# A fused attention and two feed-forward layers: P5 after P7 in FFN 1's slots, v loaded half a block earlier, one block's cosine taken unreduced, bounds in borrowed PSUM tiles, GpSimd passes cut in two

## The chip, the cores and the metric

The kernel runs on one NeuronCore of a Trainium2 chip. The metric is the device time of one execution in microseconds (us). The engines are TensorE (PE, with its weight loads shown as PEld), VectorE (DVE), ScalarE (ACT), GpSimd (POOL) and SyncE (SP), which here only issues DMAs. Each engine works through its own list of instructions in order; semaphores make an instruction wait for others. Matmuls write to PSUM, the accumulator memory; GpSimd works on SBUF only.

## The reference

Everything is float32, with N = 6016 tokens and C = 256 channels:

```python
qn = q / (norm(q, axis=1) + 1e-6);  kn = k / (norm(k, axis=1) + 1e-6)
a = softmax(kn.T @ qn / tau)          # 256 x 256: attention over channels
x = v @ a                             # 6016 x 256
h = x @ w_in1;  x = (h * cos(h)) @ w_out1        # FFN 1, d_ff = 2048
h = x @ w_in2;  out = (h * sigmoid(h)) @ w_out2  # FFN 2, d_ff = 2048
```

The weights come in as 64-bit words (seen as int64) that the kernel decodes to float32 itself.

## The kernel before, in words

**Precision.** A float32 number is split into a high part hi (fp32r, made by ScalarE's Copy) and a low part lo = x - hi (VectorE or GpSimd). A product is three passes, hi*hi, lo*hi and hi*lo (`PASSES`).

**Stages.** (1) Scores and softmax; the attention matrix is folded into `w_in1`, so that FFN 1 reads v directly. (2) FFN 1 of blocks 0 to 2, 24 units of 256 hidden columns: the 16 units of blocks 0 and 1 in turns (`TURNS`), then the 8 of block 2 (`FIRST`). A unit is 12 matmuls of 512 columns for h (`emit_h`, L727), a cosine, a split into hi and lo, and 12 matmuls into the output accumulator (`emit_o1`, L759), two units later. (3) FFN 1 of blocks 3 to 10, 8 slots each, in a Strassen-like form: seven products P1 to P7 of 128x256 per slot in place of eight (`first_layer`, L962), three passes each. Block 11 (`PLAIN`, 384 tokens) follows without that form. (4) FFN 2 of all blocks, seven products for both layers. Blocks are 512 tokens.

**The cosine.** Blocks 0 to 2 reduce the argument first: ScalarE writes k = round(h / 2 pi + 0.25) as an integer (L734), VectorE h - 2 pi k (L735), ScalarE the sine (L742), VectorE the product with h (L743). From block 3 on `cosine_in` takes the sine of h itself (L1221) times `small[b]`, which is 1 where a bound on |h| is below 1.5 and 0 otherwise, and VectorE multiplies (L1222). The bound is a small matmul (L426) of `most` (per channel, the largest |v| of a block; `span_of`, L399) and `widest` (the largest |w| of each row; L408, L417), reduced by VectorE (L430, L431). `every` gathers whether all bounds held (L432); it decides at the end whether a general version is run.

**A slot of FFN 1** (slot j; u is the pair whose products begin, p the one of slot j-1). In PSUM each pair has `ys` (y in half 1, the first sum in half 0) and `xz` (z in half 0, x in half 1). TensorE's order: P4 and P5 of p; P1 and P7 of u; the 12 output matmuls of the pair three slots back; P3 of p; P2 and P6 of u. ScalarE's: the split hi of slot j-2's pair (L1228), y <- x (L1276), p7 <- z (L1277), sine of xz (L1221), the slot's share of other work, sine of ys (L1221), u2 <- y (L1310). VectorE's: z += u2 and ys0 = y + p7 (L1012), the split lo (L1230), the product with xz (L1222), other work, the product with ys (L1222). P5 adds to y, and so waits until L1310 has copied y into u2:

```python
product(z, "P4", w, x, start=False)
product(y, "P5", w, x, start=False)   # waits for u2 <- y, the last work of ScalarE's slot
add(z, z, u2)
add(ys[k][:, 0], y, p7)
```

`p7` and `u2` are single tiles (`seeds`), used again in every slot.

**The other work** of a block's 8 slots is dealt out by `misc(b, m)`: at m = 0 and 4 a piece of `w_in2` or `w_out2` begins to be decoded (ACT L310, POOL L287), at 1 and 5 VectorE clamps it (L293, L294), at 2 and 6 VectorE and GpSimd finish it (L300, L303, L351), GpSimd splits it (L357, L358) and SP stores it (L1057). At m = 0 the v of the next block is loaded (`load_v`, L393, one buffer); at 1 to 3 it is formed and split for the seven products (POOL L906, ACT L913, L917); at m = 3 the span of v is taken, and FFN 1's finished block is copied (L825 to L827), formed (L848 to L852), split (L839, L843) and stored (L845) at m = 3 to 7. At m = 7 the next block's bound is computed into `xz`. While block 2 runs, GpSimd also forms and splits `w_in1` (A and B in `FORMING`, L929 to L944) and the v of block 3.

The order of each engine's list is the order of the code: nothing is scheduled afterwards. What a buffer's earlier reader or writer holds back waits by semaphore.

Of the kernel before, what the change touches and what calls it, by code (L numbers as in the profile page):

```python
# [217 lines left out]
def direct(ctx, tc, qk, vT, tau, w_in1, w_out1, w_in2, w_out2, outT, dp, kept, within):  # L218
# [1258 lines left out]
```

## Time and profile before

| | |
|---|---|
| median of 3 runs | 1082.03 us (1078.99 to 1083.86) |
| the profiled execution | 1083.9 us, of which 1082.1 us are the span from the first to the last instruction |
| mean granted TensorE clock | 0.980 |
| TensorE / VectorE / ScalarE / GpSimd busy | 94% / 82% / 72% / 38% of the span |

The busy shares are means over stages with different limits, so the stages have to be read one by one. TensorE's share counts matmuls at their modelled ends, and a matmul at a lower clock counts as longer.

### The profile page before, as it was taken

How to read it: one execution, taken by the hardware profiler on the slowest of the kernel's cores; microseconds unless marked ns; L12 is line 12 of the kernel's file. 1: busy time of each engine (PE TensorE's matmuls, PEld its weight loads, DVE VectorE, ACT ScalarE, POOL GpSimd, SP SyncE). 2: the span in 40 equal slices, each digit the busy share in tenths (PEclk: the TensorE clock that was granted, in tenths of full speed). 3: DMA queues.
4: the chain of work that ended last, by engine and by line, in shares of the span. 5: the costliest groups of instructions: out<-in, count | busy, mean ns of one | idle time of the engine just before them, and what ended most of it. 6: DMA issues, size and time to landing. Idle time of an engine off the chain costs nothing.

```text
span 1082.1 us, 18543 instructions
## 1 busy us (share of the span) xinstructions
PE 1015.9 (94%) x7060; PEld 945.6 (87%) x7060; DVE 891.4 (82%) x1241; ACT 783.5 (72%) x1381; POOL 413.5 (38%) x378
## 2 busy tenths in 40 slices
PE   9999998798989898898889999999999999999998
PEld 8778887687878787787878999999999999999998
DVE  6799889786878787787978568999999999999972
ACT  6886767575667666676756678888888888888863
POOL 4343358566666656566645201111111111111110
PEclk9999999898989998999999999999999999999999
DMA  9930035323233332323234985022202201220101
GB/s 350 350 125 1 1 151 229 146 88 117 89 120 124 131 142 76 140 88 117 89 112 163 364 344 185 11 79 89 87 12 79 89 27 70 81 89 12 54 22 37
DMA packets 35011, 126.58 MB, mean 117 GB/s; under 512 B 3170, under 2 KB 4450, under 8 KB 30178
## 3 DMA queue, kind: packets, MB, share of 16 engines
q1 hardware_dynamic: 34770, 125.12, 31.5%
q8 instruction: 57, 0.93, 0.4%
q14 instruction: 40, 0.33, 0.1%
q10 hardware_dynamic: 144, 0.20, 0.1%
HBM read 73.01 MB, written 52.30 MB: 116 GB/s over the span
## 4 chain that ended last, share of the span: by engine, by line
PE 63%; DVE 10%; POOL 9%; ACT 7%; DMA 6%; issue 4%; SPq 0%; POOLq 0%; ACTq 0%; DVEq 0%
PE o L962 19%; PE xz L962 12%; PE o L759 11%; PE ys L962 10%; DMA vraw<-vT_dram 5%; PE h L727 4%; DVE t L1222 2%; ACT hi L1228 2%; DVE lo L1230 2%; ACT t L1221 2%; POOL stage L358 2%; POOL t L843 2%; DMA qk<-qk_dram 1%; PE o L1002 1%; PE S L537 1%
## 5 line engine op out<-in xcount | busy, mean ns | idle before, releaser
L789 DVE TENSOR_TENSOR lo<-t,hi 128x768 fp32r<-128x768 f32 (+1 forms) x176 | 194.6, 1115 | 29.2 <-ACT hi L781 29.1
L759 PE MATMUL o<-hi,wo 128*128 128x512 f32 (+1 forms) x768 | 203.2, 389 | 0.3 <-ACT hi L748 0.3
L776 POOL TENSOR_TENSOR t<-t 128x256 f32<-128x256 f32 x88 | 64.4, 732 | 361.6 <-DVE t L773 317.7
L781 ACT ACTIVATE hi<-t 128x768 fp32r<-128x768 f32 (+1 forms) x176 | 168.9, 960 | 27.1 <-PE o L962 26.3
L759 PEld LDWEIGHTS o<-hi,wo 128*128 128x128 f32 x768 | 145.0, 198 | 18.2 <-ACT hi L748 0.9
L1230 DVE TENSOR_TENSOR lo<-t,hi 128x1024 fp32r<-128x1024 f32 (+1 forms) x72 | 113.3, 1573 | 44.1 <-ACT hi L1228 43.9
L962 PE MATMUL o<-hi,wo 128*128 128x256 f32 x770 | 134.7, 275 | 0.0
L1228 ACT ACTIVATE hi<-t 128x1024 fp32r<-128x1024 f32 (+1 forms) x72 | 74.6, 1037 | 72.7 <-DVE t L1222 64.4
L962 PE MATMUL ys<-xhi,wf 128*128 128x256 f32 x384 | 81.9, 296 | 45.9 <-ACT u L1310 45.4
L759 PE MATMUL o<-lo,wo 128*128 128x512 f32 (+1 forms) x384 | 116.1, 385 | 3.0 <-DVE lo L749 3.0
L962 PEld LDWEIGHTS ys<-xhi,wf 128*128 128x128 f32 x384 | 63.4, 192 | 61.8 <-ACT u L1310 58.1
L962 PEld LDWEIGHTS o<-hi,wo 128*128 128x128 f32 x770 | 117.0, 192 | 0.0
L962 PE MATMUL o<-lo,wo 128*128 128x256 f32 x385 | 105.9, 275 | 0.0
L759 PEld LDWEIGHTS o<-lo,wo 128*128 128x128 f32 x384 | 74.3, 195 | 14.5 <-DVE lo L749 4.0
L1222 DVE TENSOR_TENSOR t<-ys,t 128x512 f32<-128x512 f32 x64 | 43.8, 684 | 41.5 <-ACT t L1221 41.5
L1221 ACT ACTIVATE t<-ys,half_pi,small 128x512 f32<-128x512 f32 x64 | 49.7, 777 | 38.4 <-PE ys L962 38.2
L962 PE MATMUL xz<-xhi,wa 128*128 128x256 f32 x384 | 76.2, 281 | 0.4 <-ACT p L1277 0.4
L962 PEld LDWEIGHTS o<-lo,wo 128*128 128x128 f32 x385 | 73.9, 192 | 0.0
L1373 ACT ACTIVATE ys<-xz 128x256 f32<-128x256 f32 x88 | 32.4, 368 | 46.4 <-PE xz L962 45.5
L962 PE MATMUL xz<-x2hi,wf 128*128 128x256 f32 x352 | 65.8, 275 | 0.0
L962 PE MATMUL xz<-x2hi,wa 128*128 128x256 f32 x352 | 65.8, 275 | 0.0
L768 DVE TENSOR_TENSOR t<-t 128x512 f32<-128x512 f32 x88 | 60.2, 684 | 0.2 <-ACT t L1416 0.2
(250 smaller groups left out, 2987.0 us busy)
## 6 DMA issues: line engine op xcount, KB each, us to landing
qk<-qk_dram SPq DMA_DIRECT2D x22, 512.0 KB, 7.6
x2hi<-xshi SPq DMA_DIRECT2D x11, 896.0 KB, 5.1
x2lo<-xslo SPq DMA_DIRECT2D x11, 896.0 KB, 7.1
wi_dram<-stage SPq DMA_DIRECT2D x8, 1024.0 KB, 4.9
wo_dram<-stage SPq DMA_DIRECT2D x8, 1024.0 KB, 4.8
vraw<-vT_dram SPq DMA_DIRECT2D x11, 512.0 KB, 7.2
outT_dram<-q SPq DMA_DIRECT2D x22, 256.0 KB, 2.0
xshi<-t SPq DMA_DIRECT2D x10, 512.0 KB, 6.7
```

Of the source, the lines that this page charges most:

```text
L727: nc.tensor.matmul(hp[:, s, :n], lhsT, rhs, start=(i == 0), stop=(i == len(todo) - 1))
L759: nc.tensor.matmul(o[:, e, :n], wo1_at(i, f)[:, e * P : (e + 1) * P], columns(parts[k][:, s, :n]), start=(f == 0 and (i, k) == PASSES[0]), ...
L768: eng.tensor_tensor(out=t[:, 4:6, :c], in0=t[:, 0:1, :c].to_broadcast([P, 2, c]), in1=t[:, 1:3, :c], op=ALU.subtract)
L776: eng.tensor_tensor(out=t[:, 7, :c], in0=t[:, 3, :c], in1=t[:, 6, :c], op=ALU.subtract)
L781: nc.scalar.activation(hi[:, sl, :c], t[:, 1:][:, sl, :c], AF.Copy)
L789: nc.vector.tensor_tensor(out=lo[:, sl, :c], in0=t[:, 1:][:, sl, :c], in1=hi[:, sl, :c].bitcast(F32), op=ALU.subtract)
L962: nc.tensor.matmul(out, w(p, ka), columns(x[r][:, kb - 1]), start=(start and i == 0), stop=(stop and i == 2), skip_group_check=True,)
L1221: nc.scalar.activation(out, h, AF.Sin, bias=half_pi, scale=small[b])
L1222: nc.vector.tensor_tensor(out=out, in0=h, in1=out, op=ALU.mult)
L1228: nc.scalar.activation(hf, tf, AF.Copy)
L1230: nc.vector.tensor_tensor(out=lf, in0=tf, in1=hf.bitcast(F32), op=ALU.subtract)
L1373: nc.scalar.activation(y2, x2, AF.Copy)
```

## The change: what it does

- In FFN 1's slots of the seven-product form, P5 of the pair before, and the addition that reads it, come after P1 and P7 of the new pair.
- v of block b+2 is loaded at m = 4 of block b (before: of b+1 at m = 0); v of block 4 is loaded ahead of the first slot.
- Block 2's units take the sine of h itself (`cosine_in`). For that its bound is computed in unit 15: the span of v in unit 13, `widest` at the end of unit 14, the spans of the weights two units earlier (`SPANS` 6).
- The bounds of blocks 2 and 3 use the PSUM tile of the unit to come (`ready`), between the two halves of the output matmuls of units 15 and 22. Block 3's bound stood ahead of the first slot of stage 3 before.
- `small` is one tile with a column for each block; `every` is one minimum at the end in place of a product after each bound. The maximum of a bound stays in PSUM.
- GpSimd's larger subtractions and one addition are cut into two instructions: the split of decoded weights (896 columns into 512 and 384), of formed v (1024 into 2 x 512), of FFN 1's formed output from block 2 on, and of the forms of `w_in1`. The raw parts of 768 columns are left as they were.

```diff
-SPANS = 8
+SPANS = 6
...
-            nc.gpsimd.tensor_tensor(out=lo, in0=src, in1=hi.bitcast(F32), op=ALU.subtract)
+            for sl in (slice(0, 4), slice(4, NU)) if len(src.shape) == 3 else (slice(0, P),):
+                nc.gpsimd.tensor_tensor(out=lo[:, sl], in0=src[:, sl], in1=hi[:, sl].bitcast(F32), op=ALU.subtract)
...
-        s = small[b] = wp.tile([P, 1], F32, tag="small", name=f"small{b}", bufs=2)
-        nc.vector.tensor_reduce(out=s, in_=to, axis=AX.X, op=ALU.max)
-        nc.vector.tensor_scalar(out=s, in0=s, scalar1=LIMIT, scalar2=1.0, op0=ALU.is_le, op1=ALU.mult)
-        nc.vector.tensor_tensor(out=every, in0=every, in1=s, op=ALU.mult)
+        most_of_all = room[:, NS : NS + 1]
+        nc.vector.tensor_reduce(out=most_of_all, in_=to, axis=AX.X, op=ALU.max)
+        nc.vector.tensor_scalar(
+            out=small[b], in0=most_of_all, scalar1=LIMIT, scalar2=1.0, op0=ALU.is_le, op1=ALU.mult
+        )
...
-        hp = next_room().tile([P, 2, TB], F32, tag="h", name=f"h{b}_{m}")
+        hp = ready.pop() if ready else h_tile(f"h{b}_{m}")
...
         def low(kind, sl):
             hi, lo = places[kind]
-            eng.tensor_tensor(out=lo, in0=t[:, sl], in1=hi.bitcast(F32), op=ALU.subtract)
+            for k in (slice(0, 2), slice(2, 4)) if kind == "formed" and b >= 2 else (slice(None),):
+                eng.tensor_tensor(out=lo[:, k], in0=t[:, sl][:, k], in1=hi[:, k].bitcast(F32), op=ALU.subtract)
...
         hp = emit_h(u)
-        t = emit_first(i, u, hp)
+        bounded = {TURNS - 1: FIRST, TURNS + 6: FIRST + 1}.get(i)
+        if bounded is not None:
+            emit_o1(units[i - LAG], parts[i - LAG], (0,))
+            ready.append(h_tile(f"bound{bounded}"))
+            bound(bounded, ready[0][:, 0])
+        if i < TURNS:
+            t = emit_first(i, u, hp)
...
-        emit_cos(u, hp, t)
+        if i < TURNS:
+            emit_cos(u, hp, t)
+        else:
+            cosine_in(b, hp, flat(T[i % 2]))
...
+        if i == TURNS - 3:
+            span_of(FIRST, vraw)
         if i == TURNS - 2:
             split_v(FIRST, vraw)()
+            spread_weights()
...
-    raws = {}
+    raws = {FIRST + 2: load_v(FIRST + 2)}
...
     def misc(b, m):
-        if b < NB and m == 0:
-            raws[b + 1] = load_v(b + 1)
+        if m == 4 and b + 2 < NB:
+            raws[b + 2] = load_v(b + 2)
...
             product(z, "P4", w, x, start=False)
-            product(y, "P5", w, x, start=False)
             add(z, z, u2)
-            add(ys[k][:, 0], y, p7)
...
             product(x2, "P1", w_, x_, start=True)
             product(z2, "P7", w_, x_, start=False)
+        if p is not None and not pp_:
+            product(y, "P5", w, x, start=False)
+            add(ys[k][:, 0], y, p7)
...
-        if j == 0:
-            bound(FIRST + 1, next_room().tile([P, 2, TB], F32, tag="h", name="bound")[:, 0])
```

What this moves on the engines. TensorE, from P6 of one slot to the output matmuls of the next (block 5, slots 1 and 2), before; `xz1`, `ys1` are the older pair's tiles, `xz0`, `ys0` the newer one's:

```order
L962 MATMUL ys1_1473<-xhi5_1904,wf0_1026 128x256 x2
L962 MATMUL ys1_1473<-xlo5_1905,wf0_1026 128x256
L962 MATMUL xz1_1474<-xhi5_1904,wa0_89 128x256 x2
L962 MATMUL xz1_1474<-xlo5_1905,wa0_89 128x256
L962 MATMUL ys1_1473<-xhi5_1904,wf0_1026 128x256 x2
L962 MATMUL ys1_1473<-xlo5_1905,wf0_1026 128x256
L962 MATMUL xz0_1425<-xhi5_1904,wa1_90 128x256 x2
L962 MATMUL xz0_1425<-xlo5_1905,wa1_90 128x256
L962 MATMUL xz0_1425<-xhi5_1904,wf1_1027 128x256 x2
```

The pairs of rows are P6, P4, P5, P1 and the start of P7. The same place on TensorE in the changed kernel:

```order
L976 MATMUL ys1_1465<-xhi5_1902,wf0_1031 128x256 x2
L976 MATMUL ys1_1465<-xlo5_1903,wf0_1031 128x256
L976 MATMUL xz1_1466<-xhi5_1902,wa0_89 128x256 x2
L976 MATMUL xz1_1466<-xlo5_1903,wa0_89 128x256
L976 MATMUL xz0_1423<-xhi5_1902,wa1_90 128x256 x2
L976 MATMUL xz0_1423<-xlo5_1903,wa1_90 128x256
L976 MATMUL xz0_1423<-xhi5_1902,wf1_1032 128x256 x2
L976 MATMUL xz0_1423<-xlo5_1903,wf1_1032 128x256
L976 MATMUL ys1_1465<-xhi5_1902,wf0_1031 128x256 x2
L976 MATMUL ys1_1465<-xlo5_1903,wf0_1031 128x256
```

P5 (the last two rows) now stands behind P1 and P7. SP's list over block 3, before (`vraw5` is block 5's v, asked for when block 4 begins, behind the stores of block 2's output):

```order
L393 DMA vraw4_1437<-vT_dram 128x2x512
L1057 DMA wi2_dram0_1546<-stage_1031 128x2048
L267 DMA raw_wi22_1548<-w_in2_dram 128x2x256
L845 DMA xshi2_1594<-hi0_501 128x768
L845 DMA xslo2_1595<-lo0_503 128x768
L1057 DMA wi2_dram1_1751<-stage_1031 128x2048
L267 DMA raw_wi23_1753<-w_in2_dram 128x2x256
L845 DMA xshi2_1594<-t0_499 128x1024
L845 DMA xslo2_1595<-t1_500 128x1024
L393 DMA vraw5_1853<-vT_dram 128x2x512
```

And SP's list there in the changed kernel:

```order
L395 DMA vraw4_1416<-vT_dram 128x2x512
L1071 DMA wi2_dram0_1543<-stage_1036 128x2048
L268 DMA raw_wi22_1545<-w_in2_dram 128x2x256
L395 DMA vraw5_1639<-vT_dram 128x2x512
L853 DMA xshi2_1592<-hi0_502 128x768
L853 DMA xslo2_1593<-lo0_504 128x768
L1071 DMA wi2_dram1_1752<-stage_1036 128x2048
```

The load has moved past four stores, one store of decoded weights and one load. VectorE in block 2's units 16 and 17, before (`h2_0` is block 2's first h):

```order
L735 SCALAR_TENSOR_TENSOR t0_499<-t0_499,h2_0_1076 128x1024
L749 TENSOR_TENSOR lo1_504<-t1_500,hi1_502 128x1024
L743 TENSOR_TENSOR t0_499<-h2_0_1076,t0_499 128x1024
L417 TENSOR_REDUCE widest_100<-largest_99 128x2
L420 MEMSET every_101 128x1
L735 SCALAR_TENSOR_TENSOR t1_500<-t1_500,h2_1_1117 128x1024
L749 TENSOR_TENSOR lo0_503<-t0_499,hi0_501 128x1024
L743 TENSOR_TENSOR t1_500<-h2_1_1117,t1_500 128x1024
```

And VectorE from the end of unit 14 to unit 16 in the changed kernel, where h of block 2's first unit stands in `bound2`:

```order
L419 TENSOR_REDUCE widest_100<-largest_99 128x2
L431 TENSOR_REDUCE bound2_1059<-bound2_1059 128x1
L432 TENSOR_SCALAR smalls_102<-bound2_1059 128x1
L742 SCALAR_TENSOR_TENSOR t1_501<-t1_501,h1_7_1040 128x1024
L756 TENSOR_TENSOR lo0_504<-t0_500,hi0_502 128x1024
L750 TENSOR_TENSOR t1_501<-h1_7_1040,t1_501 128x1024
L756 TENSOR_TENSOR lo1_505<-t1_501,hi1_503 128x1024
L1085 TENSOR_TENSOR t0_500<-bound2_1059,t0_500 128x1024
```

The reducing pass (L735) is gone from block 2's units, and the bound's two small instructions stand one unit ahead of them.

## Rows read from the trace of the kernel before

**Rows 1.** Busy time by stretch: bounds, length, PE, PEld, DVE, ACT, POOL, PEclk, DMA

```profile
144.78:198.42 53.64, 45.31 (x200) 38.01 (x198) 49.73 (x44) 37.39 (x41) 39.55 (x25) 0.95 0.59 229
198.42:245.17 46.75, 41.84 (x253) 36.91 (x253) 35.23 (x47) 30.23 (x54) 27.82 (x27) 0.95 0.25 91
245.17:543.80 298.63, 261.97 (x1598) 235.10 (x1597) 233.31 (x313) 196.51 (x342) 187.18 (x175) 0.95 0.32 112
543.80:586.54 42.74, 38.09 (x233) 34.01 (x232) 33.64 (x49) 28.97 (x51) 17.92 (x19) 0.96 0.46 164
586.54:626.20 39.66, 38.87 (x231) 37.07 (x230) 23.22 (x34) 22.35 (x35) 16.25 (x14) 1.00 0.80 302
626.20:1082.10 455.90, 450.77 (x3927) 450.02 (x3925) 394.55 (x629) 362.31 (x748) 64.42 (x88) 1.00 0.21 77
```

**Rows 2.** Waits over the span: total us, times, longest

```profile
PEld ys L962 <- ACT u L1310: 58.1, 64, 4.4
```

**Rows 3.** Timeline of TensorE, one slot (block 8): start, length, engine, line

```profile
471.69 0.49 PE L962 MATMUL ys<-xhi,wf 128*128 128x256 f32 x2 [0.20 <-ACT u L1310]
...
472.12 0.39 PE L962 MATMUL xz<-xhi,wa 128*128 128x256 f32 x2
...
472.80 1.03 PE L759 MATMUL o<-hi,wo 128*128 128x512 f32 x4
...
475.39 0.38 PE L962 MATMUL ys<-xhi,wf 128*128 128x256 f32 x2
...
476.39 0.39 PE L962 MATMUL xz<-xhi,wa 128*128 128x256 f32 x2
...
477.09 0.49 PE L962 MATMUL ys<-xhi,wf 128*128 128x256 f32 x2 [0.20 <-ACT u L1310]
```

**Rows 4.** Timeline of ScalarE, the end of the same slot

```profile
475.92 0.78 ACT L1221 ACTIVATE t<-ys,half_pi,small 128x512 f32<-128x512 f32 x1 [0.84 <-PE ys L962]
476.65 0.38 ACT L1310 ACTIVATE u<-ys 128x256 f32<-128x256 f32 x1
```

**Rows 5.** Timeline of VectorE, the same slot

```profile
471.33 0.69 DVE L1222 TENSOR_TENSOR t<-ys,t 128x512 f32<-128x512 f32 x1 [0.53 <-ACT t L1221]
...
473.15 1.23 DVE L1230 TENSOR_TENSOR lo<-t,hi 128x1024 fp32r<-128x1024 f32 x1 [0.40 <-ACT hi L1228]
474.38 0.69 DVE L1222 TENSOR_TENSOR t<-xz,t 128x512 f32<-128x512 f32 x1
```

**Rows 6.** Timeline of SP, ScalarE and TensorE, first slots of block 8

```profile
449.43 1.88 SPq L393 DMA_DIRECT2D vraw<-vT_dram  x1
...
457.35 0.90 ACT L913 ACTIVATE xhi<-vraw 128x768 fp32r<-128x768 f32 x1 [3.91 <-DMA vraw<-vT_dram]
...
459.24 0.79 PE L962 MATMUL ys<-xhi,wf 128*128 128x256 f32 x2 [3.71 <-ACT u L1310]
```

**Rows 7.** Timeline of GpSimd and VectorE; VectorE's groups from 245.17 to 543.80

```profile
496.53 2.38 POOL L843 TENSOR_TENSOR t<-y,t 128x1024 fp32r<-128x1024 f32 x1
...
497.50 2.48 DVE L1230 TENSOR_TENSOR lo<-t,hi 128x1024 fp32r<-128x1024 f32 x1 [0.46 <-ACT hi L1228]
...
L1230 DVE TENSOR_TENSOR lo<-t,hi 128x1024 fp32r<-128x1024 f32 x48 | 81.7, 1701 | 19.4 <-ACT hi L1228 19.2
...
L432 DVE TENSOR_TENSOR every<-every,small 128x1 f32<-128x1 f32 x7 | 11.2, 1598 | 0.2
```

**Rows 8.** Block 2: timeline of TensorE; VectorE's group from 144.78 to 198.42

```profile
178.25 0.70 PE L759 MATMUL o<-lo,wo 128*128 128x512 f32 x2 [2.12 <-DVE lo L749]
...
186.95 1.03 PE L727 MATMUL h<-xhi,wa 128*128 128x512 f32 x4
...
192.13 0.20 PE L426 MATMUL bound<-most,widest 128*128 128x4 bf16 x2
197.40 0.58 PE L1147 MATMUL ys<-wo 128*128 128x256 f32 x1 [5.06 <-DVE small L430]
...
L735 DVE SCALAR_TENSOR_TENSOR t<-t,h 128x1024 f32<-128x1024 int32 x9 | 10.9, 1215 | 3.4 <-ACT t L734 3.4
```

More of the change, by code (lines that the diff above doesn't have):

```diff
@@ L249, in direct @@
     every = wp.tile([P, 1], F32, name="every")
-    small = {}
+    smalls = wp.tile([P, NB], F32, name="smalls")
+    small = {b: smalls[:, b : b + 1] for b in range(NB)}
     class Weights:
@@ L419, in spread_weights @@
         )
-        nc.vector.memset(every, 1.0)
     def bound(b, room):
@@ L717, in quadrant, with h_tile @@
         return first[name, m][:, i] if (name, m) in first else w[:, i, NU]
+    ready = []
+    def h_tile(name):
+        return next_room().tile([P, 2, TB], F32, tag="h", name=name)
     def emit_h(u):
@@ L917, in raw_low, with formed_low @@
             nc.scalar.activation(hi[:, FORMED], formed, AF.Copy)
-        return [form, raw_low, lambda: sub(lo[:, FORMED], formed, hi[:, FORMED].bitcast(F32))]
+        def formed_low():
+            for k in (slice(0, 2), slice(2, 4)):
+                sub(lo[:, FORMED][:, k], formed[:, k], hi[:, FORMED][:, k].bitcast(F32))
+        return [form, raw_low, formed_low]
     formed_w1 = {}
@@ L928, in form_w1 @@
         hi, lo = [wa[k][:, i].bitcast(F32) for i in range(2)]
-        nc.gpsimd.tensor_tensor(out=base, in0=hi, in1=lo, op=ALU.add)
+        for m in range(2):
+            nc.gpsimd.tensor_tensor(out=base[:, m], in0=hi[:, m], in1=lo[:, m], op=ALU.add)
         q = base.rearrange("p m (s b) -> p m s b", b=P)
@@ L943, in split_w1 @@
         nc.scalar.activation(hi, t, AF.Copy)
-        nc.gpsimd.tensor_tensor(out=lo, in0=t, in1=hi.bitcast(F32), op=ALU.subtract)
+        for m in range(2):
+            nc.gpsimd.tensor_tensor(out=lo[:, m], in0=t[:, m], in1=hi[:, m].bitcast(F32), op=ALU.subtract)
     def w1_slot(m):
@@ L1067, in fetch, with cosine_in @@
         nc.sync.dma_start(out=to.bitcast(F32), in_=src[:, :, : to.shape[2]])
+    def cosine_in(b, h, out):
+        nc.scalar.activation(out, h, AF.Sin, bias=half_pi, scale=small[b])
+        nc.vector.tensor_tensor(out=out, in0=h, in1=out, op=ALU.mult)
     FIRST = 2
@@ L1101, in direct @@
             vraw = load_v(FIRST)
+        if i == TURNS - 3:
+            span_of(FIRST, vraw)
         if i == TURNS - 2:
             split_v(FIRST, vraw)()
+            spread_weights()
         if i == TURNS - 1:
             vraw = load_v(FIRST + 1)
-        if i == TURNS:
-            spread_weights()
         if SPANS <= i < SPANS + 8:
@@ L1116, in direct @@
                 {"A": form_w1, "B": split_w1}[what[0]](int(what[1]))
-        if i == TURNS + 5:
+        if i == TURNS + 4:
             span_of(FIRST + 1, vraw)
@@ L1122, in direct @@
             v = units[i - LAG]
-            emit_o1(v, parts.pop(i - LAG))
+            emit_o1(v, parts.pop(i - LAG), (0, 1) if bounded is None else (1,))
             if v[1] == NPAIR - 1:
@@ L1178, in seven @@
         return t.rearrange("p s c -> p (s c)").rearrange("p (i s e) -> p i s e", i=2, s=NU)
-    raws = {}
+    raws = {FIRST + 2: load_v(FIRST + 2)}
+    del vraw
     def misc(b, m):
-        if b < NB and m == 0:
-            raws[b + 1] = load_v(b + 1)
+        if m == 4 and b + 2 < NB:
+            raws[b + 2] = load_v(b + 2)
         if m in (0, 4):
@@ L1218, in bank @@
         return t.rearrange("p j c -> p (j c)")[:, :n]
-    def cosine_in(k, b, h, out):
-        nc.scalar.activation(out, h, AF.Sin, bias=half_pi, scale=small[b])
-        nc.vector.tensor_tensor(out=out, in0=h, in1=out, op=ALU.mult)
     def high_and_low(j, q, what):
@@ L1282, in first_layer @@
         elif p is not None:
-            cosine_in(k, p[1], xz[k], tq[:, 1])
+            cosine_in(p[1], xz[k], tq[:, 1])
         if j == 0:
@@ L1307, in first_layer @@
         if p is not None and not pp_:
-            cosine_in(k, p[1], ys[k], tq[:, 0])
+            cosine_in(p[1], ys[k], tq[:, 0])
         if not up:
@@ L1321, in tail_of_first @@
             late = [sp.tile([P, NU, HB], F32R, name=f"late{k}") for k in range(2)]
+            nc.vector.tensor_reduce(out=every, in_=smalls[:, FIRST:], axis=AX.X, op=ALU.min)
             nc.vector.tensor_copy(within, every[0:1])
```

## The prediction

> **What bounds the kernel now.** I read the busy times by stretch first, then the list of waits, then the timeline of one slot on three engines. The stretches [rows 1] divide the span. The last, FFN 2, is 455.90 us with TensorE busy for 450.77 at a granted clock of 1.00; no instruction of it is changed, so it stays. The change works between 144.78 (block 2's first unit) and 626.20 (FFN 2's first product). There TensorE has gaps, and the list of waits gives their owner: its weight loads wait 58.1 us, 64 times, for L1310, the copy u2 <- y [rows 2], once for each of the 64 slots of the seven-product form.
>
> An ordinary slot shows why [rows 3]. P5 starts at 471.69 and the next P5 at 477.09: a period of 5.40. The matmuls alone are shorter. P1 starts at 472.12 and P4 at 476.39, 4.27 later without a gap; P1 and P7 take 0.68 together (472.12 to 472.80), so a product takes 0.34, and with P4 and P5 a slot is 4.27 + 0.67 = 4.94. The other 0.46 is a loop: P5, P1, P7, the 12 output matmuls to 475.39, P3, then ScalarE's sine of ys at 475.92 and u2 at 476.65 [rows 4], then the next P5. Eight floors of 4.94 are 39.5 a block. Blocks 4 to 9 take 298.63 us [rows 1], 49.8 each. Of the 10.3 above the floor, eight loops are 3.7, and the first slots of a block give 3.7 more: v is asked for at 449.43, ScalarE waits 3.91 us for it at 457.35, and P5, which needs ScalarE's u2, has waited 3.71 at 459.24 [rows 6]. The remaining 2.9 is what follows the gap (the granted clock is 0.95 over these blocks and 1.00 in FFN 2, and the first two matmuls behind it take 0.79 against 0.49 in rows 3), and late VectorE work.
>
> VectorE is late where GpSimd is in its way. A lo takes 1.23 us alone [rows 5]; at 497.50 it takes 2.48, having met a GpSimd subtraction of 2.38 that began at 496.53 [rows 7]. Over 48 lo the mean is 1701 ns [rows 7], so the excess is 0.47 x 8 = 3.8 us a block. In the first stretch, block 2's, an undisturbed unit is 192.13 - 186.95 = 5.18 [rows 8], eight are 41.4; the stretch is 53.64 long.
>
> **The change part by part.**
>
> *P5 behind P7.* The loop loses P1 and P7: 5.40 - 0.68 = 4.72, under the floor of 4.94, so TensorE is what is late next and an ordinary slot gains 0.46. The price could be on the other side of P5: the addition that reads p7 now follows P7, and ScalarE may not write the next p7 before it. P5 would start 1.0 us after P4, and its three matmuls (0.34) and an addition shorter than the 0.69 of the 512-column product [rows 5] end by about 2.1. ScalarE's hi ends at about the same time (473.15, when lo begins [rows 5], is 2.1 after that slot's P4, which stands one period before 476.39 [rows 3]), and the copy of y stands between hi and p7: a margin of some tenths. I take nothing for it, with 0.3 a slot as the upper end.
>
> *v half a block earlier.* The one buffer is free by then, its last reader being VectorE's span at m = 3. In SP's list the load stands behind the m = 2 store of weights and ahead of the stores of FFN 1's output. v took 457.35 - 449.43 = 7.9 us to be usable [rows 6], and now has more than four slots (over 19 us). So the 3.7 us goes whole, and the low clock with it. For block 4's v, asked for just before the first slot, SP first has the stores of block 1's output; I leave 1 us of wait in block 3.
>
> *GpSimd's passes in two, and no product into `every`.* L432 goes, 11.2 us in the six blocks or 1.9 each [rows 7]. A lo that meets a pass waits for half as long at most, but there are more passes to meet. Bounds: nothing to 1.9 (half of 3.8) a block; I take 1. The additional passes cost GpSimd perhaps 0.1 us each; it is busy for 187.18 of 298.63 us, so that is hidden.
>
> Here a rule speaks against the change. The row at 497.50 shows that the lo ended 1.07 us after GpSimd's pass (499.98 against 498.91), as if it had begun then [rows 7]. The Trainium skill, "SBUF — State Buffer", section "Who interferes with whom", says that a VectorE instruction with two SBUF inputs and a GpSimd instruction that reads SBUF exclude each other for the whole instruction; the trace agrees, as the numbers before this sentence show. By that rule cutting a pass in two leaves the time for which the pair is taken as it was; that is the first rival.
>
> *Sum for a block.* TensorE's floor is 39.5. VectorE is busy for 233.31 / 6 = 38.9; less 1.9 for L432 and 1 for shorter meetings 36.0, and it idles 0.40 a slot for hi [rows 5], 3.2 in eight: 39.2. Both chains are so near each other that uneven slots (the forms of x2 and the clamp fall into m = 4 and 5, one after another) will show; I add 2.5 to the floor: 42.0 a block. Blocks 4 to 9: 6 x 7.8 = 46.6 saved. Block 10's first seven slots [rows 1]: 42.74 - 7 x 5.25 = 6.0. The stretch behind has one such wait and a few: 0.8. Block 3 (46.75) has three short slots, since its output matmuls are block 2's last two units: 4.38 + 3.64 + 3.64 + 5 x 4.94 = 36.4 as a floor (a product 0.335, 12 output matmuls 2.59 from rows 3); the VectorE chain makes the short ones about 1 us longer each, and with 1.1 for uneven slots and 1 for v it is 40.5: 6.2 saved.
>
> *Block 2.* Each of eight units loses one ScalarE and one VectorE pass (L735, 1215 ns [rows 8]); VectorE is busy for 49.73 of this stretch's 53.64 us [rows 1], and TensorE's waits there are for its lo (2.12 at 178.25 [rows 8]). With 9.7 us less it is no longer the bound. Block 3's bound stood between block 2 and block 3: TensorE did it at 192.13 and waited 5.06 us for VectorE's answer behind other work, up to 197.40 [rows 8]. Now it stands a unit earlier, between two halves of output matmuls, with the answer needed 1.3 us later. Block 2's own bound comes in unit 15, behind the span and the spread, which VectorE does in units that now have two more reductions; for a late answer there I allow from nothing to 1 us. Floor 41.4 + 0.44 (clear, P1) = 41.9; with 1.6 for the two bounds and the meetings with GpSimd, which is busy for 39.55 of the 53.64 us, 43.5: 10.1 saved. What GpSimd has left over (the last `w_in1` forms) is needed only by slot 6.
>
> *Total.* 10.1 + 6.2 + 46.6 + 6.0 + 0.8 = 69.7. The span would be 1012.4, the execution (1.8 us around the span) 1014.2. The profiled execution lies 1.9 above the median, so the forecast is 1012.3, say 1013.
>
> **The rivals.**
>
> *The pair of GpSimd and VectorE becomes the bound.* GpSimd's 31.2 us a block (187.18 / 6, some of it waiting) and VectorE's eight lo at 1.23 add to 41.0 without VectorE's decoding and forms. If these exclude each other wholly and instructions wait for each other besides, a block is 46: 22.6 saved in blocks 4 to 9, 3 in block 10, 3 in block 3, 7 in block 2; 1083.9 - 35.6 - 1.9 = 1046. For it: 41.0 is above 39.5. Against: GpSimd has 18.6 us a block in which it is not busy, and its results are needed a slot or more later. 0.12.
>
> *The wait moves to ScalarE.* p7 is one tile: L1277 now waits for the addition behind P5, the sines come late and with them u2. At 0.3 a slot, and a little for v's return, a block is 44.5: 6 x 5.3 + 4 + 4 + 10 = 50 saved, 1032. For it: the margin worked out above is a few tenths, and any late P5 uses it up. Against: ScalarE still has 0.84 of idle before the sine of ys [rows 4]. 0.15.
>
> *TensorE nearly at its floor.* Blocks of 40.3, block 3 at 38, block 2 at 42.5: 57 + 8.7 + 11.1 + 7.5 + 1 = 85 saved, 997. For it: the loop of 4.72 has slack in every slot, which can take up one late slot. Against: the two chains of 39.5 and 39.2. 0.15.
>
> *Slower.* GpSimd's chain falls behind the block. Its place is ScalarE's L310 at m = 0 and 4, which needs a buffer that GpSimd must first have emptied (two buffers for decoding and for formed v), and stands ahead of the sine of ys. While GpSimd's work for a block, waits included, is under a block's length, L310 waits at most once; from 49.8 us on each block is as long as GpSimd's work, and what it exceeds that by is lost. It has 31.2 now and would need 18.6 more, fifteen further meetings at the 1.23 of a lo, where a block has eight lo. At 52 a block, with blocks 3 and 10 as they were: 6 x 2.2 = 13 lost, less the 10 of block 2: 1085. Against it is that the added passes are no added work. 0.02. (If block 2's bound failed, the general version would run as well; worked out from the reference's inputs that bound is 0.90 against the limit of 1.5.)
>
> **How the numbers follow.** The forecast, 1013, has 0.56, with its own range of 1003 to 1024. The others have 0.12, 0.15, 0.15 and 0.02. From 1000 to 1036 lies the forecast, the wait on ScalarE and a part of the floor case: 8 in 10. Within 0.5% (5.4 us, about what a measurement of this kernel can tell from no change) would need 64 us of the gain to be lost: 0.02; slower 0.02; faster 0.96.
>
> **What would show it.** Right: slots of 4.94 to 5.0 in a block's middle, L913 without a wait for v, no gap at L1147 ahead of the first slot, the clock at 0.98 or more in blocks 4 to 9, and the wait for L1310 from 58 us down to under 15. Wrong: slots of 5.2 and more with ScalarE idle ahead of L1277 for VectorE's addition; lo still at 1.6 us in the mean with slots of 5.7; GpSimd busy for over 90% of a block; a gap at unit 15 ahead of the bound; more than 66 us saved with blocks near 40, which would say that I over-counted the two chains' disturbance.

## The result, and the profile after

The changed kernel takes 1032.38 us (median of 4 runs, 1031.59 to 1033.43) against 1082.94 for the kernel before on the same chip: ratio 0.9539, 95% interval 0.9511 to 0.9567. It is faster by 50.6 us; forecast were 70 and a time of 1013, with a range of 1000 to 1036. The measured time lies in that range, but above the 1003 to 1024 that the prediction gave as the forecast's own. The profiled execution has a span of 1029.8 us, 52.3 less than before.

Busy time by stretch, changed kernel, columns as in [rows 1]: block 2, block 3, blocks 4 to 9, block 10's first seven slots, what lies behind up to FFN 2, FFN 2.

```profile
145.09:188.99 43.90, 43.07 (x200) 36.46 (x199) 31.25 (x30) 27.71 (x32) 34.93 (x26) 1.00 0.61 241
188.99:238.72 49.73, 40.74 (x251) 36.19 (x250) 35.67 (x49) 32.00 (x56) 38.58 (x36) 0.97 0.36 130
238.72:499.11 260.39, 245.70 (x1599) 224.64 (x1597) 215.98 (x307) 196.53 (x342) 208.38 (x199) 1.00 0.37 128
499.11:534.22 35.11, 34.99 (x233) 32.48 (x232) 30.96 (x45) 28.18 (x49) 20.39 (x20) 1.00 0.48 166
534.22:573.65 39.43, 39.20 (x233) 37.52 (x232) 22.52 (x37) 23.41 (x37) 18.99 (x18) 1.00 0.78 312
573.65:1029.80 456.15, 450.79 (x3927) 450.03 (x3925) 394.66 (x629) 362.30 (x748) 64.44 (x88) 1.00 0.21 78
```

Beside [rows 1] this is the whole account of the 52.3 us:

| stretch | before | after | saved | forecast |
|---|---|---|---|---|
| ahead of block 2 | 144.78 | 145.09 | -0.31 | 0 |
| block 2 | 53.64 | 43.90 | 9.74 | 10.1 |
| block 3 | 46.75 | 49.73 | -2.98 | 6.2 |
| blocks 4 to 9 | 298.63 | 260.39 | 38.24 | 46.6 |
| block 10, seven slots | 42.74 | 35.11 | 7.63 | 6.0 |
| behind it | 39.66 | 39.43 | 0.23 | 0.8 |
| FFN 2 | 455.90 | 456.15 | -0.25 | 0 |

Two stretches miss by 9.2 and 8.4 us; the others are within 1.7.

The -0.31 ahead of block 2 hides two opposite amounts. FFN 1's first unit began 1.28 us earlier in this execution (54.42 against 55.70; the executions profiled here begin it between 54.38 and 56.24), and unit 15, which now holds block 2's bound, takes 6.47 (138.62 to 145.09) where it took 5.19 (139.59 to 144.78). Timeline of TensorE in unit 15, changed kernel:

```profile
138.62 1.03 PE L734 MATMUL h<-xhi,wa 128*128 128x512 f32 x4
...
143.64 0.20 PE L427 MATMUL bound<-most,widest 128*128 128x4 bf16 x2 [0.97 <-DVE widest L419]
...
145.09 1.03 PE L734 MATMUL bound<-xhi,wa 128*128 128x512 f32 x4
```

The bound's matmul waits 0.97 us for VectorE's `widest`.

**An ordinary slot** is at TensorE's floor. Timeline of TensorE and ScalarE, block 8 of the changed kernel, answering to [rows 3] and [rows 4]: P5, P3, u2 on ScalarE, the next P5 and the output matmuls behind it.

```profile
412.64 0.39 PE L976 MATMUL ys<-xhi,wf 128*128 128x256 f32 x2
...
415.57 0.38 PE L976 MATMUL ys<-xhi,wf 128*128 128x256 f32 x2
...
416.83 0.38 ACT L1336 ACTIVATE u<-ys 128x256 f32<-128x256 f32 x1
...
417.57 0.39 PE L976 MATMUL ys<-xhi,wf 128*128 128x256 f32 x2
...
417.91 1.03 PE L766 MATMUL o<-hi,wo 128*128 128x512 f32 x4
```

P5 comes every 4.93 us with no wait; u2 is written from 416.83, well before P5 at 417.57. Of a block's eight slots four take 4.93 or 4.94. From P7 to P7, block 8's are 4.94, 4.93, 5.84, 4.93, 4.94, 6.76, 5.19, 5.86: 43.39. Each block from 4 to 9 repeats them within 0.05, so the longer ones have fixed causes. The list of waits (total us, times, longest; [rows 2] before):

```profile
PEld ys L976 <- ACT u L1336: 17.9, 18, 1.8
...
ACT wf L956 <- POOL w1form L950: 13.4, 3, 6.0
...
ACT wv_wi L311 <- POOL stage L360: 9.7, 4, 2.4
...
ACT wv_wo L311 <- POOL stage L360: 7.4, 3, 2.5
```

The 58.1 us of [rows 2] are 17.9, and below them stand two waits of ScalarE for GpSimd, at L956 and at L311 (a row each for the pieces of `w_in2` and `w_out2`). L311's makes the slot of 6.76, at m = 4 to 5. Timeline of GpSimd, ScalarE and TensorE, changed kernel:

```profile
437.65 0.61 POOL L360 TENSOR_TENSOR stage<-wv_wo,stage 128x128 fp32r<-128x128 f32 x1
...
438.29 0.66 ACT L311 ACTIVATE wv_wo<-raw_wo 128x512 f32<-128x512 f32 x1 [2.44 <-POOL stage L360]
438.86 0.76 ACT L1084 ACTIVATE t<-ys,half_pi,smalls 128x512 f32<-128x512 f32 x1
439.52 0.36 ACT L1336 ACTIVATE u<-ys 128x256 f32<-128x256 f32 x1
...
439.94 0.49 PE L976 MATMUL ys<-xhi,wf 128*128 128x256 f32 x2 [1.56 <-ACT u L1336]
```

L311 begins a decode into a buffer that GpSimd empties only at 438.26. It stands ahead of the sine of ys in ScalarE's list, so the sine, u2 and P5 wait with it. The slot of 5.84, at m = 2 to 3, is a meeting of VectorE and GpSimd; the same view:

```profile
423.97 1.87 POOL L914 TENSOR_TENSOR xlo<-vraw,xhi 128x768 fp32r<-128x768 f32 x1
...
424.31 2.61 DVE L1255 TENSOR_TENSOR lo<-t,hi 128x1024 fp32r<-128x1024 f32 x1 [0.45 <-ACT hi L1253]
426.84 0.68 DVE L1085 TENSOR_TENSOR t<-xz,t 128x512 f32<-128x512 f32 x1
...
427.57 0.49 PE L976 MATMUL xz<-xhi,wa 128*128 128x256 f32 x2 [0.64 <-DVE t L1085]
```

The lo takes 2.61, where one alone takes 1.23 [rows 5]; the product with xz behind it is late, and P1 may not overwrite xz before that. GpSimd's pass is one of the raw parts of 768 columns, which the change left whole.

**Block 3's first slot** takes 11.67 us. Timeline of GpSimd, ScalarE and TensorE there:

```profile
195.28 0.72 POOL L950 TENSOR_TENSOR w1form<-w1base,w1form 128x256 f32<-128x256 f32 x1
196.04 1.06 ACT L956 ACTIVATE wf<-w1form 128x1024 fp32r<-128x1024 f32 x1 [6.00 <-POOL w1form L950]
...
197.30 0.36 ACT L1303 ACTIVATE p<-xz 128x256 f32<-128x256 f32 x1
...
197.72 0.80 PE L976 MATMUL xz<-xhi,wa 128*128 128x256 f32 x2 [4.79 <-ACT p L1303]
```

ScalarE's split of the last `w_in1` form (L956) belongs to block 2's last unit and waits 6.00 us for GpSimd; slot 0's y and p7 stand behind it, and TensorE waits 4.79 us for them.

### The profile page after: what moved, and what is told of

It is laid out like the page before. It is cut to its first block, busy times and chain, and to the rows that moved or that the text cites. A ratio compares the mean times of both kernels' runs of the same rounds, so it can differ in the third digit from the quotient of the medians.

```text
span 1029.8 us, 18600 instructions
## 1 busy us (share of the span) xinstructions
PE 994.8 (97%) x7062; PEld 932.1 (91%) x7062; DVE 855.1 (83%) x1227; ACT 775.7 (75%) x1373; POOL 445.3 (43%) x419
## 4 chain that ended last, share of the span: by engine, by line
PE 68%; POOL 11%; ACT 7%; DVE 6%; issue 6%; DMA 2%; SPq 0%; DVEq 0%; POOLq 0%; ACTq 0%
PE o L976 20%; PE xz L976 14%; PE o L766 12%; PE ys L976 12%; PE h L734 3%; POOL stage L360 3%; DVE t L1085 2%; ACT t L1084 2%; ACT hi L1253 2%; PE o L1016 2%; DMA qk<-qk_dram 1%; PE S L539 1%; POOL w1base L942 1%; POOL stage L358 1%; POOL w1form L950 1%
## 5 line engine op out<-in xcount | busy, mean ns | idle before, releaser
L766 PE MATMUL o<-hi,wo 128*128 128x512 f32 (+1 forms) x768 | 194.2, 376 | 0.3 <-ACT hi L755 0.3
L766 PEld LDWEIGHTS o<-hi,wo 128*128 128x128 f32 x768 | 138.7, 190 | 15.6 <-ACT hi L755 0.7
L1255 DVE TENSOR_TENSOR lo<-t,hi 128x1024 fp32r<-128x1024 f32 (+1 forms) x72 | 107.8, 1497 | 39.8 <-ACT hi L1253 39.8
L976 PEld LDWEIGHTS o<-hi,wo 128*128 128x128 f32 x770 | 117.0, 192 | 0.0
L766 PE MATMUL o<-lo,wo 128*128 128x512 f32 (+1 forms) x384 | 113.0, 376 | 1.1 <-DVE lo L756 1.1
L976 PE MATMUL ys<-xhi,wf 128*128 128x256 f32 x384 | 76.3, 281 | 14.4 <-ACT u L1336 14.3
L976 PEld LDWEIGHTS ys<-xhi,wf 128*128 128x128 f32 x384 | 63.3, 192 | 21.3 <-ACT u L1336 17.9
L766 PEld LDWEIGHTS o<-lo,wo 128*128 128x128 f32 x384 | 72.0, 189 | 11.7 <-DVE lo L756 2.6
L976 PEld LDWEIGHTS o<-lo,wo 128*128 128x128 f32 x385 | 74.0, 192 | 0.0
L976 PEld LDWEIGHTS xz<-xhi,wa 128*128 128x128 f32 x384 | 58.8, 194 | 13.8 <-DVE t L1085 6.9
L1084 ACT ACTIVATE t<-ys,half_pi,smalls 128x512 f32<-128x512 f32 x64 | 49.8, 778 | 15.1 <-PE ys L976 14.0
```

The lines of the kernel that those rows point to most:

```text
L766: nc.tensor.matmul(o[:, e, :n], wo1_at(i, f)[:, e * P : (e + 1) * P], columns(parts[k][:, s, :n]), start=(f == 0 and (i, k) == PASSES[0]), ...
L976: nc.tensor.matmul(out, w(p, ka), columns(x[r][:, kb - 1]), start=(start and i == 0), stop=(stop and i == 2), skip_group_check=True,)
L1255: nc.vector.tensor_tensor(out=lf, in0=tf, in1=hf.bitcast(F32), op=ALU.subtract)
```

## The experiments

All twelve change the changed kernel, except the last two, which change the kernel before. Times are medians; ratios are to the kernel before in the same set (1082.87, 1082.05 or 1083.52), and a difference of times between sets is uncertain by the 1.5 us between these. For the first and the third run the interval of the ratio overlaps the changed kernel's (0.9511 to 0.9567), but their lowest times, 1036.96 and 1036.20, lie above its highest, 1033.43. Block 2's own parts of the change (the unreduced cosine, the two bounds) and the product into `every` were not taken back one by one: what is said of them rests on the stretches and rows.

**P5 put back.** P5 and its addition stand behind P4 again, as in the kernel before:

```diff
             product(z, "P4", w, x, start=False)
+            product(y, "P5", w, x, start=False)
             add(z, z, u2)
+            add(ys[k][:, 0], y, p7)
```

> The changed kernel with P5 and its addition put back ahead of P1 and P7, all else as changed. Theory (the loop over u2 was 5.40 us and P5's move took P1 and P7, 0.68 us, out of it): the five slots of a block that now take 4.94 go back to 5.40, those that GpSimd makes late stay, so a block goes from 43.4 to about 46 and the time from 1032 to about 1050. Rival (the move only carried the wait from TensorE to ScalarE's copy into p7, and the gain came from the load of v alone): about 1032.

1037.80 us (1036.96 to 1040.21), 0.9577 [0.9553, 0.9600]. Blocks 4 to 9 take 264.83 against 260.39, 44.1 each. Six of eight slots are at 5.40, so the loop is what the slot view says. But the slot with L311 falls from 6.77 to 5.6: longer slots give GpSimd the time that ScalarE waited for, and L311's longest wait in blocks 4 to 9 is 0.5 us. The order of P5 is worth 5.4 us here, not 29 (64 slots of 0.46); the time agrees with neither expectation.

**v loaded at m = 0 again.**

```diff
-    raws = {FIRST + 2: load_v(FIRST + 2)}
+    raws = {}
...
-        if m == 4 and b + 2 < NB:
-            raws[b + 2] = load_v(b + 2)
+        if b < NB and m == 0:
+            raws[b + 1] = load_v(b + 1)
```

> The changed kernel with v of the next block loaded at m = 0 again, all else as changed. Theory (the wait for v was 3.7 us a block, with a low clock behind it): about 5 us in each of seven blocks come back, 1032 to about 1065. Rival (the load only ended in time because the slots wait for GpSimd anyway): 1035 to 1045, since GpSimd's other work would fill the wait.

1078.40 us (1076.66 to 1079.09), 0.9957 [0.9941, 0.9973]: v's early load is worth 46 us in the changed kernel, more than expected. Blocks 4 to 9 take 298.76 us, the 298.63 of before, with four slots at 4.93 or 4.94 and the third at 12.3 to 13.4. Its waits:

```profile
POOL vform L914 <- DMA vraw<-vT_dram: 44.6, 7, 7.4
ACT xhi L921 <- DMA vraw<-vT_dram: 39.2, 7, 6.9
```

So what the other slots gave, v's wait took back.

**GpSimd's passes whole again.** All the cuts in two are undone, in this manner:

```diff
-            for k in (slice(0, 2), slice(2, 4)):
+            for k in (slice(None),):
```

> The changed kernel with GpSimd's passes in one piece again, all else as changed. Theory (a lo waits at most for the rest of one pass, so that halves are worth about 1 us a block): 1036 to 1043. Rival (GpSimd and VectorE exclude each other for the same total in halves, so that halves are worth nothing): 1030 to 1034.

1037.30 us (1036.20 to 1038.93), 0.9571 [0.9547, 0.9596], as the theory had it. Blocks 4 to 9:

```profile
241.68:505.63 263.95, 252.40 (x1598) 226.51 (x1597) 229.14 (x307) 196.29 (x342) 199.77 (x175) 1.00 0.36 126
```

Against the third row of the stretches, VectorE is busy 13.2 us longer and GpSimd 8.6 us shorter. Cutting moves time of the meetings from VectorE, which TensorE waits for, to GpSimd. Most of it is at one place, which the expectation did not name. VectorE's groups in blocks 4 to 9, with whole passes and then in the changed kernel:

```profile
L1253 DVE TENSOR_TENSOR lo<-t,hi 128x1024 fp32r<-128x1024 f32 x48 | 79.0, 1645 | 17.2 <-ACT hi L1251 17.2
...
L859 DVE TENSOR_TENSOR y<-y 128x256 f32<-128x256 f32 x6 | 14.8, 2466 | 0.2
```

```profile
L1255 DVE TENSOR_TENSOR lo<-t,hi 128x1024 fp32r<-128x1024 f32 x48 | 76.9, 1602 | 17.0 <-ACT hi L1253 17.0
...
L859 DVE TENSOR_TENSOR y<-y 128x256 f32<-128x256 f32 x6 | 2.6, 426 | 0.6
```

Of the 13.2 us, 12.2 are L859, an addition that forms FFN 1's output: it met the split of formed v, a single pass of 2.80 us. The lo account for 2.1, and another addition, L856, takes 1.0 back. Blocks 4 to 9 give 3.6 us of the difference in time; in the profiled executions another 1.8 are in unit 15, where the bound waits 1.83 for VectorE.

**Decode begun later.** L311 of m = 4 goes behind u2 in ScalarE's list:

```diff
-        if m in (0, 4):
-            W = raws["W"] = next(coding)
-            W.decode_first()
+        if m == 0:
+            begin_decode()               # the same two lines
...
             nc.scalar.activation(u2, y2, AF.Copy)
+            if u[2] == 4:
+                begin_decode()
```

> The changed kernel with the start of decoding at m = 4 (ScalarE's first pass and GpSimd's) moved to the end of its slot, behind the copy u2 <- y. Theory (the slot of 6.77 us in each block is ScalarE's first decoding pass, which waits 2.4 us for the buffer that GpSimd empties, ahead of the sine and u2): that slot falls to about 5.1, a block from 43.4 to about 41.7, the time to about 1021. Rival (GpSimd and VectorE exclude each other for so long in a block that the delay shows up in another slot): a block of 43.4 still, 1032.

1019.69 us (1019.14 to 1019.78), 0.9411 [0.9389, 0.9433]. The slot of 6.77 is 5.05, the next one 4.94 in place of 5.2, and the blocks take 41.4 (248.63 in all): with the decode begun later the time is 12.7 us less, 11.8 of it in blocks 4 to 9. L311 still waits, 0.5 us at most in blocks 4 to 9, but the sine and u2 now stand ahead of it. The edit also moves GpSimd's first pass (L288) behind its L860; that was not tried apart.

**`w_in1`'s forms earlier.**

```diff
-FORMING = {15: 'A0', 16: 'B0', 17: 'A1', 18: 'B1 V', 19: 'V', 20: 'V A2', 21: 'B2', 22: 'A3', 23: 'B3'}
+FORMING = {15: 'A0 A1', 16: 'B0', 17: 'B1 A2', 18: 'V', 19: 'V B2', 20: 'V', 21: 'A3', 22: 'B3'}
```

> The changed kernel with the forming of w_in1 dealt out earlier over block 2's units (A0 A1 in unit 15, then B0, B1 A2, V, V B2, V, A3, B3 in units 16 to 22), so that GpSimd uses the 11 us in which it is idle around 140 to 151. Theory (block 3's first slot takes 11.7 us because ScalarE's split of the last form stands ahead of the slot's copies and waits 6.0 us for GpSimd): the wait goes, the first slot is 4.5 to 6, the time 1024 to 1027. Rival (TensorE would then wait there for block 4's v, asked for late, or for VectorE): the first three slots together gain less than 2 us, 1030 to 1032.

1033.44 us (1031.49 to 1035.49), 0.9548 [0.9520, 0.9576]: no gain; the rival's reason is right, and the time is 1.4 above what it gave. The first slot falls from 11.67 to 6.63, the third rises from 5.79 to 10.97. Timeline of SP, ScalarE and TensorE:

```profile
195.36 0.32 SPq L853 DMA_DIRECT2D xslo<-t  x1
195.73 1.52 SPq L395 DMA_DIRECT2D vraw<-vT_dram  x1
...
203.51 0.90 ACT L921 ACTIVATE xhi<-vraw 128x768 fp32r<-128x768 f32 x1 [4.66 <-DMA vraw<-vT_dram]
...
205.40 0.79 PE L976 MATMUL ys<-xhi,wf 128*128 128x256 f32 x2 [4.83 <-ACT u L1336]
```

Block 4's v, asked for behind the stores of block 1's output, is 4.66 us late. In the changed kernel the first wait hid all but 1.08 us of it.

**GpSimd's raw parts in thirds.** The two subtractions of 768 columns become three of 256 each:

```diff
-            sub(turned(lo, RAW), q[:, 1:], turned(hi, RAW).bitcast(F32))
+            for k in range(3):
+                sub(turned(lo, RAW)[:, k], q[:, 1 + k], turned(hi, RAW)[:, k].bitcast(F32))
```

(and the same for L851.)

> The changed kernel with the two raw subtractions of GpSimd that it left whole (768 columns, 1.9 us each a block) cut into three. Theory (the slots of 5.84 at m = 2 and of 5.2 and 5.85 at m = 6 and 7 are VectorE instructions that met one of these): each of the two places loses about 0.6 us, a block is 42.2, the time 1023 to 1027. Rival (the two engines exclude each other for the same total, however it is cut): 1030 to 1033.

1022.27 us (1021.13 to 1024.02), 0.9444 [0.9417, 0.9471]: below the rival's, and 0.7 under the lower end of what the theory gave. The slots of 5.84 and 5.19 become 4.94, the one of 5.86 becomes 5.36; 6.7 to 6.9 stays. Blocks 4 to 9:

```profile
238.16:488.91 250.75, 240.95 (x1598) 223.06 (x1597) 203.57 (x307) 198.27 (x342) 222.25 (x223) 1.00 0.38 132
```

VectorE is busy 12.4 us less, GpSimd 13.9 us more.

**Decode later and forms earlier**, both edits:

> The start of decoding at m = 4 behind u2 (as in the run before) and the forming of w_in1 dealt out earlier. Theory: the two gains are in different stretches and add, 1019.7 - 6.5, about 1013. Rival (GpSimd's time is the bound, and what is taken from it in one place comes back in another): above 1017.

1020.18 us (1019.43 to 1020.23), 0.9417 [0.9393, 0.9441]. The forms add nothing to the later decode, and the time is the rival's, but not for its reason: blocks 4 to 9 keep what they gained, while block 3 takes 48.89 us, its third slot 11.71, much like the 10.97 with the forms alone.

**All three edits** (decode, forms, thirds):

> The same two and GpSimd's raw subtractions in three. Theory: a block of about 40.3, 1004 to 1009. Rival (the pair shared by GpSimd and VectorE is the bound of a block at about 41): blocks stay at 41.4, the time at 1012 to 1014.

1013.72 us (1012.79 to 1016.78), 0.9369 [0.9341, 0.9397]. Blocks 4 to 9 fall to 40.9 us, 245.32 in all, between the theory's 40.3 and the rival's 41.4. The time is the rival's and misses the theory's by 5 to 10, mostly since block 3 still takes 46.01, 10.28 of them in its third slot.

**All three, and block 4's v asked for two units before block 2 ends:**

```diff
+        if i == TURNS + 5:
+            vnext = load_v(FIRST + 2)
...
-    raws = {FIRST + 2: load_v(FIRST + 2)}
+    raws = {FIRST + 2: vnext}
```

> The kernel of all three edits, and block 4's v is asked for two units before block 2 ends, as soon as block 3's v has been read, in place of just before the first slot of block 3. Theory (the late v of block 4 is all that is left in block 3): the wait of ScalarE for it in the third slot goes, block 3 falls from 46.0 to about 40.5 us, and the time to 1008 us (1006 to 1010). Rival (the third slot waits for GpSimd, which forms block 4's v and still has pieces of w_in1 to do): the third slot stays near 10 us, the time at 1013.

1010.42 us (1008.31 to 1011.04), 0.9325 [0.9299, 0.9351], the fastest kernel of the study, though its interval overlaps that of the three edits. Its blocks 3 and 4 to 9:

```profile
191.14:233.27 42.13, 39.44 (x252) 34.88 (x251) 36.35 (x50) 32.57 (x57) 33.13 (x34) 1.00 0.42 150
233.27:478.84 245.57, 243.56 (x1599) 223.98 (x1598) 208.90 (x307) 197.01 (x342) 221.94 (x223) 1.00 0.39 135
```

The third slot is 4.93, so the late v was its cause. Block 3 gains 3.9 us and is 42.13, where about 40.5 was expected; the median gains 3.3 and is 0.4 above the 1006 to 1010. Block 2 is 0.5 us longer than in the changed kernel (44.41 against 43.90), as in the other runs with the earlier forms. It also starts later, at 146.74 in place of 145.09, but FFN 1's first unit had begun 1.8 us later already (56.24 against 54.42), so that is no cost of the edits.

**Forms and v for block 3 alone**, on the changed kernel:

> The changed kernel with both edits for block 3 alone: the forms of w_in1 dealt out earlier and block 4's v asked for two units before block 2 ends. Theory (two waits stand one behind the other, and each alone takes what the other gives): block 3 falls from 49.7 to 41 us and the time from 1032.4 to 1024 (1022 to 1027). Rival (something else in block 3's first slots, GpSimd's load above all, is the limit): block 3 at 46 or more, the time above 1028.

1028.57 us (1027.43 to 1029.47), 0.9501 [0.9476, 0.9526]. Block 3 falls from 49.73 to 44.36, between the two expectations, and the time is just inside the rival's. Both waits are gone; the first three slots, 6.63, 4.13 and 6.05, still hold about 5 us above the prediction's floor of 11.66 for them (4.38 + 3.64 + 3.64), in part waits of the output matmuls for ScalarE and VectorE (1.08 and 0.64 in the first), and their cause was not tried. With block 2 starting 1.3 us later and 0.5 us longer in the profiled execution, 3.6 of the 5.4 remain. The interval of the ratio overlaps the changed kernel's, so that this gain is read from the stretch.

**v's load alone, on the kernel before:**

```diff
-    raws = {}
+    raws = {FIRST + 2: load_v(FIRST + 2)}
...
-        if b < NB and m == 0:
-            raws[b + 1] = load_v(b + 1)
+        if m == 4 and b + 2 < NB:
+            raws[b + 2] = load_v(b + 2)
```

> The kernel before with one part of the change alone: v asked for at m = 4 of the block before last. Theory (v's wait is the largest part of the change, and the parts do not just add up): the first slots of blocks 4 to 9 lose their gap, the clock rises, the other slots stay at the loop of 5.40, a block is 44.5 to 45.5 us in place of 49.8, the time 1045 to 1052. Rival (as the prediction had it, 3.7 us a block and something for the clock): a block at 46 or more, the time 1055 to 1062.

1052.62 us (1051.61 to 1054.59), 0.9725 [0.9698, 0.9752], 0.6 above what the theory gave, and under the rival's. Blocks 4 to 9:

```profile
244.93:515.73 270.80, 250.50 (x1599) 225.76 (x1597) 229.82 (x313) 197.78 (x342) 196.25 (x175) 1.00 0.35 123
```

Against [rows 1], 27.8 us less, 4.6 a block, at a granted clock of 1.00 in place of 0.95. Most slots are 5.40, the first and the seventh of a block 6.0 to 6.2.

**P5's move alone, on the kernel before** (the reverse of the first experiment):

> The kernel before with one part of the change alone: P5 and the addition behind it moved behind P1 and P7. Theory (while v comes late, the wait for it takes back what shorter slots give, since v is asked for at a block's start and the work behind it is due at a fixed time later): a block stays between 48.5 and 50 us, the time between 1074 and 1084. Rival (each of 64 slots gains its 0.46 us, whatever else waits): 1053 to 1060.

1084.11 us (1081.42 to 1085.36), 1.0007 [0.9993, 1.0021]: the edit that takes the loop out of 64 slots changes nothing by itself. Blocks 4 to 9 take 301.38 us, 50.2 each, at a clock of 0.94; both are a little above what the theory gave. Timeline of SP, ScalarE, GpSimd and TensorE in block 8, and the next block's load:

```profile
447.75 2.38 POOL L843 TENSOR_TENSOR t<-y,t 128x1024 fp32r<-128x1024 f32 x1
450.16 0.50 SPq L845 DMA_DIRECT2D xslo<-t  x1
450.71 1.77 SPq L393 DMA_DIRECT2D vraw<-vT_dram  x1
...
458.41 0.90 ACT L913 ACTIVATE xhi<-vraw 128x768 fp32r<-128x768 f32 x1 [6.78 <-DMA vraw<-vT_dram]
458.53 1.64 POOL L906 TENSOR_TENSOR vform<-vraw 128x256 f32<-128x256 f32 x2 [7.40 <-DMA vraw<-vT_dram]
...
460.30 0.80 PE L962 MATMUL ys<-xhi,wf 128*128 128x256 f32 x2 [5.93 <-ACT u L1311]
...
498.74 2.38 POOL L843 TENSOR_TENSOR t<-y,t 128x1024 fp32r<-128x1024 f32 x1
...
501.70 1.78 SPq L393 DMA_DIRECT2D vraw<-vT_dram  x1
```

This is a loop with the length of a block. v's load stands on SP's queue behind the store of x2's low part, which waits for GpSimd's L843. GpSimd waits 7.40 us for v, then does the block's forms, decoding and splits in its order, waits for VectorE and ScalarE included, 42.6 us in all, until the next L843 ends at 501.12; then come the stores and the next load at 501.70, 50.99 after the last. In the kernel before the same two loads are 449.43 and 499.49, 50.06 apart. TensorE's shorter slots do not shorten it: from v's arrival to the end of L843 are 42.59 us here and 41.44 in the kernel before (457.47 to 498.91), and the wait for v is longer (5.93 against 3.71 in [rows 6]). Of the 42.59, 10.3 are GpSimd's waits for VectorE and ScalarE, whose work follows the slots; how much of the loop these set was not tried apart.

## Why the prediction was right or wrong

**Right:** the sign, the time inside the range, and the mechanisms of most steps. That the range holds the time is in part luck: it reached up to 1036 to cover the rival with the wait on ScalarE's p7, put at 1032, and the measured 1032.38 got there by other waits, 19 us above the forecast. P5 behind P7 makes an ordinary slot 4.94. v's wait is gone in blocks 4 to 9, and the granted clock there is 1.00. Block 2 saved 9.74 for 10.1 forecast: L735 is gone, VectorE is busy 31.25 us of the stretch in place of 49.73, and in place of the gap at L1147 [rows 8] the matmul of that line starts at 188.53 at once. VectorE is busy 36.0 us a block in blocks 4 to 9 (215.98 / 6), as forecast. The rival with the wait on ScalarE's p7 did not come: TensorE waits for p7 once, in block 3's first slot, and there behind L956; ScalarE's copy into p7 waits once for VectorE's addition, 0.4 us.

**Signs.** The wait for u2 fell to 17.9 us, not under 15. Of the signs of being wrong two came in part: lo is at 1.60 us in the mean, with slots of 5.84 and 5.86 in each block, and there is a gap at unit 15 ahead of the bound. That gap is 0.97 us and unit 15 is 1.28 longer, at or a little above the upper end of the 0 to 1 us allowed for block 2's bound.

**Wrong, 9.2 us: block 3.** Two sentences failed. "What GpSimd has left over (the last `w_in1` forms) is needed only by slot 6" asked when the result is read, not what stands behind the waiting instruction. L956 is on ScalarE's list ahead of slot 0's copies, and when block 2 got 9.7 us shorter GpSimd's forms did not. And "I leave 1 us of wait in block 3" for v was 1.08, but only because the other wait covered it: with the forms dealt out earlier it was 4.66. The two run beside each other, so dealing out the forms earlier gave nothing alone, and with v asked for earlier as well it gave 5.4 us (v earlier alone was not run). The other 3.8 stay open. The sum for block 3 was off besides: its terms (36.4, three short slots about 1 us longer each, 1.1 and 1) add to 41.5, not 40.5.

**Wrong, 8.4 us: the 2.5 us for uneven slots** in "42.0 a block", which were 3.9 (43.40 - 39.5). Two causes were measured: L311's wait, 11.8 us of blocks 4 to 9 when the decode is begun later alone, and the meetings with the raw parts, 9.6. Together they are 15.1, not the sum; both act on the slots at m = 5 and 6. Of the 1.4 a block that stay, most is at m = 7, where the next block's bound is computed, which was not tried apart. L311's place and its buffer are in the prediction, but in the rival for slower, as a loss only from 49.8 us a block on. It doesn't need that. GpSimd has slack over a block and is still late at one point of it, and an instruction that waits in a list kept in order costs there.

**Wrong though the sum hides it: the gains were added up per slot.** The terms 0.46 x 8 for P5 and 3.7 and more for v were taken as independent. P5's move alone was worth 0, v's load alone 30.9 us, P5's with everything else in place 5.4. While v comes late the loop over a block sets the time and the slots' gain becomes wait; once v is early the slots count, and of their gain L311's wait takes the most (its slot is 6.77 where it was 5.6 with the longer slots). The prediction's rows had the sign of it, in that [rows 6] shows ScalarE waiting where the slots are already at 5.40, but I followed the wait to v's load and not on to what let the load start.

**GpSimd's passes in two** were put at 1 us a block with a bound of 1.9, and the mean of lo fell from 1701 [rows 7] to 1602 ns, 0.8 us a block. That fit is in part chance: with whole passes, all else as changed, lo are at 1645, so that the halves give 0.3 of it; they took 2.0 a block from the addition L859 instead, which the prediction doesn't name. TensorE's blocks gained 0.6 each. The rule of the Trainium skill ("SBUF — State Buffer", "Who interferes with whom") that the pair exclude each other for the whole instruction agrees with the trace: the lo at 424.31 ends 1.08 us after GpSimd's pass. But what I concluded from it in the first rival, that a cut leaves the time as it was, did not hold for TensorE: whole passes cost 4.9 us, thirds of the raw parts gave 10.1; over six blocks cutting took 13.2 and 12.4 us from VectorE's busy time and added 8.6 and 13.9 to GpSimd's. The pair may be taken about as long as before, which was not measured by itself; who waits for it changes.

## What to carry to other kernels

Before two gains are added, follow each wait back until the chain closes on itself: here v's load was let go by a store that waited for work on the v before it, a loop of one block, and no faster slot could show until that was cut. Where an engine's list is kept in order, ask of an instruction that waits what stands behind it, not only when its result is needed; here moving one of ScalarE's waits, for GpSimd work that nothing needed soon, gave 12.7 us, more than the 5.4 of the removed loop. Work of an engine with slack that blocks one without can be worth cutting into short instructions, even if it makes the first engine busier; look which instruction of the other engine meets it.

## What the runs showed of the hardware

The granted clock follows the gaps. With TensorE waiting about 4 to 6 us once in a block, blocks 4 to 9 run at 0.93 to 0.95; with v early they run at 1.00, though slots still hold waits of 1.6 us. With whole passes a single wait of 1.83 us, in unit 15, was followed by a granted clock of 0.50 from 146.50 to 149.70. The first product behind block 3's gap of 4.79 us takes 0.80 for two matmuls that take 0.39 in an ordinary slot; the granted clock there, from 197.72 to 198.90, is 0.50, the 1.2 GHz level of the two. Pieces of 256 columns on GpSimd add 13.9 us to its own busy time over six blocks, while VectorE loses 12.4.
